# Weight bits of two halves in one operation, other due times for an inverse and a split, and no constant products

## The chip, the cores and the metric

The kernel runs on one core of a Trainium2 chip. The metric is the device time of one execution in microseconds. The kernel before took 1024.21 us, the median of three runs (1024.08 to 1024.55).

The engines have these names: PE does the matmuls (PEld is its loading of weights), DVE is the vector engine, ACT the scalar engine, POOL is GpSimd, and SP issues most DMAs. Each engine works through its own list of instructions in order, and waits where an instruction needs what another engine has not finished.

## The reference

Three stages follow each other, on 4 x 768 tokens:

```
for t in range(S):                          # attention, B=4 H=8 S=768 D=48
    kt, vt, bt = k_n[:, :, t], v[:, :, t], beta[:, :, t, None]
    y[:, :, t] = einsum('bhd,bhde->bhe', q[:, :, t], state)
    v_old = einsum('bhde,bhd->bhe', state, kt)
    state = state + bt[..., None] * einsum('bhd,bhe->bhde', kt, vt - v_old)
x = y as 3072 x 384
h = x @ w_in                                # first network, 384 x 2048
P = a[0] + a[1]*h + a[2]*h*h + a[3]*h*h*h
Q = 1 + abs(b[0])*abs(h) + abs(b[1])*h*h
x = (P / (Q + 1e-6)) @ w_out                # 2048 x 384
h = x @ w_in2; r = maximum(h, 0)            # second network
result = (r * r) @ w_out2
```

The rows k_n are k divided by its length. The weights reach the chip as 64-bit floats, and the kernel makes 32-bit floats of them.

## The kernel before

**Attention.** The recurrence is rewritten by chunks of the sequence. Each of six groups (g = 0 to 5) needs the inverse of triangular 32x32 blocks: 31 pairs of steps (L545 multiplies into tmp, L549 adds into Tt), on DVE for the first group and on POOL for the others. Then come merges of the inverses on PE (L623 and L637: products of TT, TN and ws) and bursts of small products by chunk (L734), which make the tokens' x. In the names of the order, Tt0 and Tt1, Gb0 and Gb1, vn0 and vn1 are the tiles of even and odd groups.

**First network.** The weight matrix is cut into NJ=16 tiles of 128 hidden units (j = 0 to 15), and the tokens into NT=6 passes of 512 (i). For every (i, j) there are four pieces:
- mm1 (L1021): nine products on PE, six of xh and three of xl with A (Aj), the weight as a high and a low half (A_hi, A_lo); x too is split in xh and xl (by DVE, L1005 for the second network).
- the rational: ACT makes |h| (L1044), the linear parts (L1048, L371), a logarithm (L1068) and an exponential (L1069); DVE makes the cubic and the end (L1057 to L1061); b*a is L1056 on POOL or DVE, L1054 on DVE for the first j. L1061 gives g.
- in the first pass, the products of g with B, the tile of w_out (L1105, plain). From the second pass on g is split in ph (ACT, L1078) and pl (L1079, POOL or DVE), and L1108 does products with E and F, the high and low part of B; F is B less E (L1099).
- output sums stay in banks 0 to 2 over all j.

**Weights (`weights`).** A weight tile has 768 numbers per partition, each in two 32-bit words, hi and lo: 384 of w_in (slice si) and 384 of w_out (slice so). ACT rescales hi (L959), ACT or DVE shifts lo by 29 (L960, L961). Then DVE puts the bits together, shift left by 3 and or, once per half: L969 for the in-half in place, L971 for the out-half into B. ACT copies the in-half to A_hi (L980), and a subtract gives A_lo (L981), on POOL or DVE. In the second network both halves are one operation in place (L975). Raw weights lie in the tiles raw, ra, rb and in slots called mem.

**Second network.** mm1 again, then relu and square (L1122, L1123, L1125, L1126), and products with C (L1135 to L1137). Its first mm1 follow the last products of the first network.

**What sets the order.** Nothing in the program's text does. Every instruction is a task in the class `Plan`, with an engine, an assumed duration and a due time. `run()` plays the tasks eight times: `play` takes on each engine the task that is due first among the ready ones, and `late` moves the due times backward from the end that came out. The order of the best round is issued, and is then fixed on each engine. A task made by `shared` goes to POOL or DVE, one made by `either` to ACT or DVE, as the assumed durations decide. `weights(1, j, ...)` gets its due times from tm(j), the time at which mm1 of tile j is planned. INV1 is the due time of the inverses of g from 2 on; WARM is half of the number of constant products (L458) that stand on PE at 36 to 47 us (each is two instructions in the trace); LAG1 is the distance from mm1 to the products of the same j.

Of the kernel before, what the change touches and what calls it, by code (L numbers as in the profile page):

```python
# [20 lines left out]
C = 64  # L21
# [11 lines left out]

T0, U1, U2 = 72.0, 5.55, 4.15
T2 = T0 + 96 * U1 + 3
STEP0, STEP1, INV0, INV1 = 28, 25, -90, -10
GD, GN = 26, 19
QS = (1, 1, 1, 1)
HELD = 14
OPEN = 4  # L40
BEHIND = 9
FUSE = 3
# [7 lines left out]
ROUNDS = 8  # L50
PREF, PREF2 = 1.0, 1.0
IV1, WB, WS, GW = 30, 30, 4.5, 1.2
WARM = 12
SA, SB = 40, 4


# [196 lines left out]
def kernel(ctx, tc, kT, kS, qT, kn, vn, beta, par_in, w1, w2, outT):  # L253
# [679 lines left out]
    def weights(l, j, due, duo, slack):  # L933
# [14 lines left out]
        def lo():  # L948
            return raw(rk).bitcast(U32).rearrange("p (n t) -> p n t", t=2)[:, :, 0]
# [4 lines left out]
        def res(s):  # L954
            return lo().bitcast(F32)[:, s] if f64 else raw(rk)[:, s]
        si, so = slice(0, DM), slice(DM, 2 * DM)
        if f64:
            held0 = early if l == 1 else []
            add("ACT", 0.9, lambda: A_.activation(hi().bitcast(F32), hi().bitcast(F32), AF.Prelu, scale=2.0 ** -112, alpha=2.0 ** 32), w=[(rk, 1)], due=d0, after=held0)  # L959
            fa = lambda: A_.activation(lo(), lo(), AF.Copy, scale=2.0 ** -29 * (1 - 2.0 ** -13), bias=7.5 * 2.0 ** -13 - 0.5)  # L960
            fv = lambda: V.tensor_scalar(lo(), lo(), 29, None, op0=ALU.logical_shift_right)  # L961
            if l == 1 and j in SHIFT:
                add("ACT", 0.95, fa, w=[rk], due=d0, after=held0)
            elif l == 1:
                add(("ACT", "DVE"), (0.95, 0.95), (fa, fv), lock=(0, 1), w=[rk], due=d0, after=held0)
            else:
                add("DVE", 0.95, fv, w=[rk], due=d0, lock=1)
        if f64 and l == 1:
            add("DVE", 0.7, lambda: V.scalar_tensor_tensor(lo()[:, si], hi()[:, si], 3, lo()[:, si], op0=ALU.logical_shift_left, op1=ALU.bitwise_or),  # L969
                r=[(rk, 1)], w=[rk], due=due, lock=1)  # L970
            add("DVE", 0.84, lambda: V.scalar_tensor_tensor(Bw(j).bitcast(U32), hi()[:, so], 3, lo()[:, so], op0=ALU.logical_shift_left, op1=ALU.bitwise_or),  # L971
                r=[rk, (rk, 1)], w=[("B", j)], due=duo, lock=1, free=[rk], after=over)
            last = [len(PL.tasks) - 1]
        elif f64:
            add("DVE", 1.15, lambda: V.scalar_tensor_tensor(lo(), hi(), 3, lo(), op0=ALU.logical_shift_left, op1=ALU.bitwise_or),  # L975
                r=[(rk, 1)], w=[rk], due=due, lock=1)
        elif l == 1:
            add("ACT", 0.55, lambda: A_.copy(Bw(j), res(so)), r=[rk], w=[("B", j)], due=duo, free=[rk], after=over)
            last = [len(PL.tasks) - 1]
        add("ACT", 0.52, lambda: A_.copy(Aw[j][:, si], res(si)), r=[rk], w=[("A", j)], due=due)  # L980
        shared(1.15, 0.9, lambda E: E.tensor_tensor(Aw[j][:, so], res(si), Aw[j][:, si], op=ALU.subtract),  # L981
               r=[rk], w=[("A", j)], due=due, free=[rk])
        if l == 1:
            used[rk] = last + [len(PL.tasks) - 1]
        if l == 2:
            used[rk] = [len(PL.tasks) - 1, len(PL.tasks) + 1]
            add("ACT", 0.52, lambda: A_.copy(late["C"][j][:, si], res(so)), r=[rk, "late"], w=[("C", j)], due=duo)
            add("POOL", 1.15, lambda: P_.tensor_tensor(late["C"][j][:, so], res(so), late["C"][j][:, si], op=ALU.subtract),
                r=[rk], w=[("C", j)], due=duo, lock=1, free=[rk])
            if j == 0:  # L990
                x2free[0] += [used[rk][0], len(PL.tasks) - 1]
# [181 lines left out]
    def swap():
        actx.close()
# [109 lines left out]
```

## Time and profile before

| | before |
|---|---|
| median of three runs | 1024.21 us |
| profiled execution | 1023.5 us |
| its span in the trace | 1021.7 us |
| PE busy | 969.0 us (95%) |
| DVE busy | 710.2 us (70%) |
| ACT busy | 621.3 us (61%) |
| POOL busy | 491.0 us (48%) |
| instructions | 23569 |

The profile cuts the span into 40 slices of 25.5 us; each digit is the busy share in tenths, and PEclk is the clock that PE was granted, in tenths of its full 2.4 GHz:

```profile
PE   5695999999999999999999989999999999999998
DVE  6868989998978889899769998963343433433332
POOL 3188995799879769965446976620000000000000
PEclk7677999999999999999999999999999999999999
```

The first four slices (to 102 us) hold the start of attention and of the first network; the slice at about 610 us, the 24th, holds the change from the first network to the second. In the last 15 slices POOL has nothing to do.

### The profile page before, as it was taken

The numbers are of one execution on the slowest core, as the hardware profiler recorded it, in microseconds if no ns is written. First come the engines' busy times: TensorE is split into PE (matmuls) and PEld (weight loads), VectorE is DVE, ScalarE is ACT, GpSimd is POOL, SyncE is SP. The second block draws the span as 40 slices with busy tenths as digits, with TensorE's granted clock in tenths as the row PEclk, the third lists the DMA queues.
The fourth block names the chain that finished last, engine by engine and source line by source line (L and its number), as shares of the span: only waits on it lengthen the run. The fifth ranks groups of instructions, "written<-read, shape, count | busy, mean of one in ns | idle before, by whom it ended". The sixth has DMA issues, their size and how long they took to land.

```text
span 1021.7 us, 23569 instructions
## 1 busy us (share of the span) xinstructions
PE 969.0 (95%) x9635; PEld 774.1 (76%) x9635; DVE 710.2 (70%) x1127; ACT 621.3 (61%) x1121; POOL 491.0 (48%) x609
## 2 busy tenths in 40 slices
PE   5695999999999999999999989999999999999998
PEld 4584566578777877787888867888888888888886
DVE  6868989998978889899769998963343433433332
ACT  3576878888886688678768885743232332323332
POOL 3188995799879769965446976620000000000000
PEclk7677999999999999999999999999999999999999
DMA  5975469214803541251111127300010100000000
GB/s 148 243 218 167 86 214 246 55 45 130 159 31 88 146 80 46 79 116 36 36 69 63 31 93 281 122 31 32 1 62 1 31 31 0 28 4 1 32 1 31
DMA packets 126668, 84.66 MB, mean 83 GB/s; under 512 B 95584, under 2 KB 111520, under 8 KB 126560
## 3 DMA queue, kind: packets, MB, share of 16 engines
q1 hardware_dynamic: 126560, 83.16, 29.7%
q8 instruction: 75, 1.23, 0.5%
q14 instruction: 33, 0.27, 0.1%
HBM read 63.54 MB, written 18.61 MB: 80 GB/s over the span
## 4 chain that ended last, share of the span: by engine, by line
PE 69%; POOL 13%; DVE 7%; ACT 4%; issue 3%; DMA 2%; SPq 0%; ACTq 0%; POOLq 0%; DVEq 0%
PE bank L1021 30%; PE bank L1108 10%; PE bank L734 7%; PE bank L1137 6%; PE bank L1135 6%; PE bank L1136 6%; POOL Tt L549 4%; POOL tmp L545 4%; POOL mem L1056 2%; POOL pl L1079 2%; PE bank L1105 2%; DVE mem L1061 1%; DVE bank L1060 1%; DVE mem L1059 1%; DVE mem L1057 1%
## 5 line engine op out<-in xcount | busy, mean ns | idle before, releaser
L1021 PE MATMUL bank<-xh,A 128*128 128x512 f32 (+1 forms) x1170 | 302.7, 394 | 16.7 <-DVE A L981 10.7
L1021 PEld LDWEIGHTS bank<-xh,A 128*128 128x128 f32 x1170 | 217.1, 190 | 72.1 <-DVE A L981 10.9
L1123 DVE SCALAR_TENSOR_TENSOR mem<-bank,mem 128x512 f32<-128x512 f32 x96 | 66.1, 689 | 147.4 <-ACT mem L1122 147.4
L1021 PE MATMUL bank<-xl,A 128*128 128x512 f32 (+1 forms) x585 | 163.7, 388 | 0.0
L1122 ACT ACTIVATE mem<-bank 128x512 f32<-128x512 f32 x96 | 57.4, 598 | 155.5 <-PE bank L1021 155.5
L1056 POOL TENSOR_TENSOR mem<-mem 128x512 f32<-128x512 f32 x84 | 109.7, 1307 | 49.3 <-ACT mem L1048 47.2
L1021 PEld LDWEIGHTS bank<-xl,A 128*128 128x128 f32 x585 | 110.0, 190 | 22.7
L1079 POOL TENSOR_TENSOR pl<-mem,ph 128x512 fp32r<-128x512 f32 x75 | 101.6, 1355 | 34.2 <-ACT ph L1078 25.0
L1126 DVE TENSOR_TENSOR gl<-mem,gh 128x512 fp32r<-128x512 f32 x96 | 71.8, 748 | 62.7 <-ACT gh L1125 62.6
L1137 PE MATMUL bank<-gh,C 128*128 128x512 f32 x288 | 113.7, 395 | 0.0
L1135 PE MATMUL bank<-gl,C 128*128 128x512 f32 x288 | 113.5, 394 | 0.0
L1136 PE MATMUL bank<-gh,C 128*128 128x512 f32 x288 | 111.9, 389 | 0.0
L1125 ACT CAST gh<-mem 128x512 fp32r<-128x512 f32 x96 | 59.6, 621 | 75.1 <-DVE mem L1123 62.5
L1108 PE MATMUL bank<-pl,E 128*128 128x512 f32 x240 | 99.7, 416 | 5.7 <-POOL pl L1079 5.2
L549 POOL TENSOR_TENSOR Tt<-Tt,tmp 128x31 f32<-128x31 f32 (+15 forms) x155 | 92.6, 597 | 9.4
L1108 PE MATMUL bank<-ph,F 128*128 128x512 f32 x240 | 94.8, 395 | 0.0
L1108 PE MATMUL bank<-ph,E 128*128 128x512 f32 x240 | 94.5, 394 | 0.0
L545 POOL TENSOR_TENSOR tmp<-Gb,Tt 128x31 f32<-128x31 f32 (+15 forms) x155 | 86.0, 555 | 9.7
L1068 ACT ACTIVATE mem<-mem,par 128x512 f32<-128x512 f32 x96 | 69.2, 721 | 27.5 <-POOL mem L1056 21.0
L1059 DVE SCALAR_TENSOR_TENSOR mem<-mem,par,bank 128x512 f32<-128x512 f32 x96 | 71.2, 742 | 18.1 <-ACT bank L1069 16.5
L1044 ACT ACTIVATE mem<-bank 128x512 f32<-128x512 f32 x96 | 56.8, 592 | 35.5 <-PE bank L1021 21.7
L1058 DVE SCALAR_TENSOR_TENSOR mem<-mem,par,bank 128x512 f32<-128x512 f32 x96 | 71.4, 744 | 2.1
(190 smaller groups left out, 1814.9 us busy)
## 6 DMA issues: line engine op xcount, KB each, us to landing
raw<-in_w_dram SPq DMA_DIRECT2D x17, 768.0 KB, 5.1
rb<-in_w_dram SPq DMA_DIRECT2D x8, 768.0 KB, 4.9
gs<-Gs SPq DMA_DIRECT2D x40, 128.0 KB, 3.2
X<-in_qT_dram SPq DMA_DIRECT2D x44, 112.0 KB, 2.9
kn<-in_kn_dram SPq DMA_DIRECT2D x12, 384.0 KB, 4.4
vn<-in_vn_dram SPq DMA_DIRECT2D x12, 384.0 KB, 4.5
y<-mem SPq DMA_DIRECT2D x18, 256.0 KB, 2.0
out_dram<-mem SPq DMA_DIRECT2D x18, 256.0 KB, 2.0
```

The source lines that it names most:

```text
L545: E_.tensor_tensor(tv, _mid(Gb[:, s, s + 1:32], [128, a, b]), Tt[:, 0:a, s:s + 1].to_broadcast([128, a, b]), op=ALU.mult)
L549: E_.tensor_tensor(Tt[:, 0:a, s + 1:32], Tt[:, 0:a, s + 1:32], tv, op=ALU.subtract)
L734: M.matmul(*y[:3], start=a, stop=z)
L1021: M.matmul(h, a, b, start=(m == 0), stop=(m == len(seq) - 1))
L1056: shared(1.32, 0.75, lambda E: E.tensor_tensor(b(), b(), a(), op=ALU.mult), r=[ak], w=[bk], due=due + 4.2)
L1059: q3 = lambda: V.scalar_tensor_tensor(c(), c(), s(0), h(), op0=ALU.add, op1=ALU.mult)
L1079: shared(1.3, 0.72, lambda E: E.tensor_tensor(slot[mk][0], g(), slot[pk][0], op=ALU.subtract), r=[gk, pk], w=[mk], due=due + 11.5, alloc=( ...
L1108: M.matmul(acc[d], a, b, start=(j == 0 and m == 0), stop=(j == NJ - 1 and m == 2))
L1126: add("DVE", 0.76, lambda: V.tensor_tensor(gl(), b(), gh(), op=ALU.subtract), r=[bk, gk, "late"], w=[lk], due=due + 5, lock=1, alloc=(("gl ...
L1135: M.matmul(acc[d], wh, gl, start=(j == 0), stop=False)
L1136: M.matmul(acc[d], wl, gh, start=False, stop=False)
L1137: M.matmul(acc[d], wh, gh, start=False, stop=(j == NJ - 1))
```

## The change

Five things change. First, for eleven of the sixteen weight tiles of the first network (j > 0 and j % 4 < 3) the bits of both halves are put together in one operation, 768 wide, in place of two of 384 (the branch `wide`, L973 of the new kernel). Its result goes into B: the out-half into slot j, and the in-half into slot j+1 behind it, from where ACT's copy and the subtract read it before the next tile's operation writes slot j+1. For that the two halves of w_in and w_out are stored the other way round (`w(..., True)`). The raw tile is free after the fused operation alone. Tiles 0, 3, 7, 11 and 15 keep their two operations. Second, the assumed duration of the subtract on DVE is 0.7 and not 0.9 (LOW). Third, INV1 goes from -10 to 20. Fourth, WARM is 0. Fifth, the products of the last pass are due 12 and not 18 behind mm1 (LAG0), and the split of x for the first pass of the second network is due 12 and not 4 ahead.

```diff
-STEP0, STEP1, INV0, INV1 = 28, 25, -90, -10
+STEP0, STEP1, INV0, INV1 = 28, 25, -90, 20
+LOW = 0.7
-WARM = 12
+WARM = 0
...
+        ra, rb = (so, si) if l == 1 else (si, so)
+        wide = f64 and l == 1 and j > 0 and j % 4 < 3
...
-        if f64 and l == 1:
-            add("DVE", 0.7, lambda: V.scalar_tensor_tensor(lo()[:, si], hi()[:, si], 3, lo()[:, si], op0=ALU.logical_shift_left, op1=ALU.bitwise_or),
+        if wide:
+            both = held("B", j // 4, f"Q{j // 4}", [128, 4 * DM], F32)[:, DM * (j % 4):DM * (j % 4) + 2 * DM]
+            add("DVE", 1.05, lambda: V.scalar_tensor_tensor(both.bitcast(U32), hi(), 3, lo(), op0=ALU.logical_shift_left, op1=ALU.bitwise_or),
+                r=[rk, (rk, 1)], w=[("B", j), ("B", j + 1)], due=due, lock=1, free=[rk], after=over)
+            last = [len(PL.tasks) - 1]
+        elif f64 and l == 1:
+            add("DVE", 0.7, lambda: V.scalar_tensor_tensor(lo()[:, ra], hi()[:, ra], 3, lo()[:, ra], op0=ALU.logical_shift_left, op1=ALU.bitwise_or),
                 r=[(rk, 1)], w=[rk], due=due, lock=1)
...
-        add("ACT", 0.52, lambda: A_.copy(Aw[j][:, si], res(si)), r=[rk], w=[("A", j)], due=due)
-        shared(1.15, 0.9, lambda E: E.tensor_tensor(Aw[j][:, so], res(si), Aw[j][:, si], op=ALU.subtract),
-               r=[rk], w=[("A", j)], due=due, free=[rk])
+        af = (lambda: both[:, so]) if wide else lambda: res(ra)
+        ak_ = [("B", j + 1)] if wide else [rk]
+        add("ACT", 0.52, lambda: A_.copy(Aw[j][:, si], af()), r=ak_, w=[("A", j)], due=due)
+        shared(1.15, LOW, lambda E: E.tensor_tensor(Aw[j][:, so], af(), Aw[j][:, si], op=ALU.subtract),
+               r=ak_, w=[("A", j)], due=due, free=[] if wide else [rk])
...
-    LAG1, LAG2 = 18.0, 12.0
+    LAG0, LAG1, LAG2 = 12.0, 18.0, 12.0
...
-            mm2_1(i, j, t + LAG1)
+            mm2_1(i, j, t + (LAG1 if i < NT - 1 else LAG0))
...
-        split(i, 2, due - 4)
+        split(i, 2, due - 4 if i else due - 12)
...
-    r["w1"] = w(moe_w_in[rows], moe_w_out)
+    r["w1"] = w(moe_w_in[rows], moe_w_out, True)
```

Lines from about 960 on have moved by 2 to 10: L961 is L964, L969 and L971 are L977 and L979, L980 and L981 are L990 and L991, L1021 is L1031, L1054 to L1061 are L1064 to L1071, L1079 is L1089 and L1108 is L1118 in the new kernel.

Since the order is made from durations and due times, it changes in many places. On DVE, in the first pass, these twelve instructions ended with the subtract of A2 before (mem slots hold raw weights or parts of the rational, A5 is j=5's tile):

```order
L961 TENSOR_SCALAR ra3_1088<-ra3_1088 128x768
L1054 TENSOR_TENSOR mem_102<-mem_102 128x512
L981 TENSOR_TENSOR A5_89<-raw1_107,A5_89 128x384
L677 TENSOR_TENSOR vn0_144<-vn0_144,nT1_140 128x768
L971 SCALAR_TENSOR_TENSOR B1_1285<-raw1_107 128x384
L971 SCALAR_TENSOR_TENSOR B0_898<-mem_102 128x384
L969 SCALAR_TENSOR_TENSOR ra2_993<-ra2_993 128x384
L969 SCALAR_TENSOR_TENSOR ra3_1088<-ra3_1088 128x384
L518 SCALAR_TENSOR_TENSOR nbr_138<-nbr_138,Gb0_128 128x32
L519 RECIPROCAL nbr_138<-nbr_138 128x32
L520 TENSOR_TENSOR nbr_138<-nbr_138,be_137 128x32
L981 TENSOR_TENSOR A2_86<-mem_102,A2_86 128x384
```

Now these stand around it on DVE, in the same place of the program:

```order
L991 TENSOR_TENSOR A0_84<-mem_102,A0_84 128x384
L973 SCALAR_TENSOR_TENSOR B1_179<-raw0_106 128x768
L838 TENSOR_TENSOR X2_123<-XQ2_111,bank6_75 112x4x48
L991 TENSOR_TENSOR A3_87<-mem_102,A3_87 128x384
L832 TENSOR_TENSOR xl_101<-bank7_76,xh_100 128x3x64
L838 TENSOR_TENSOR X3_124<-XQ3_112,bank5_74 112x4x48
L964 TENSOR_SCALAR ra2_984<-ra2_984 128x768
L832 TENSOR_TENSOR xl_101<-bank3_72,xh_100 128x3x64
L964 TENSOR_SCALAR ra3_1078<-ra3_1078 128x768
L991 TENSOR_TENSOR A2_86<-B0_178,A2_86 128x384
L979 SCALAR_TENSOR_TENSOR B0_178<-mem_102 128x384
L1064 TENSOR_TENSOR mem_102<-mem_102 128x512
```

The subtract of A2 comes 16 instructions earlier, counted from the same cast of x; the subtract of A5 and the scaling of vn0 have left DVE.

On POOL, where the second inverse (Tt1) ends, the third (Tt0) followed at once before:

```order
L545 TENSOR_TENSOR tmp1_133<-Gb1_129,Tt1_131 128x31
L549 TENSOR_TENSOR Tt1_131<-Tt1_131,tmp1_133 128x31
L545 TENSOR_TENSOR tmp0_132<-Gb0_128,Tt0_130 128x31
L549 TENSOR_TENSOR Tt0_130<-Tt0_130,tmp0_132 128x31
L545 TENSOR_TENSOR tmp0_132<-Gb0_128,Tt0_130 128x60
```

Now four instructions that were on DVE stand between the two inverses on POOL:

```order
L546 TENSOR_TENSOR tmp1_133<-Gb1_129,Tt1_131 128x31
L550 TENSOR_TENSOR Tt1_131<-Tt1_131,tmp1_133 128x31
L991 TENSOR_TENSOR A4_88<-B1_179,A4_88 128x384
L678 TENSOR_TENSOR vn0_144<-vn0_144,nT1_140 128x768
L678 TENSOR_TENSOR vn1_145<-vn1_145,nT1_140 128x768
L991 TENSOR_TENSOR A5_89<-B1_179,A5_89 128x384
L546 TENSOR_TENSOR tmp0_132<-Gb0_128,Tt0_130 128x31
L1066 TENSOR_TENSOR mem_102<-mem_102 128x512
```

The subtracts of A4 and A5 and both scalings of vn come behind the last step of the second inverse, and the first b*a on POOL behind the first step of the third.

On PE, at the change of the networks, the first mm1 of the second (A0) came behind the first third of j=14's products (pl0, ph0) before:

```order
L1108 MATMUL bank0_69<-pl0_2607,E3_3526 128x512
L1108 MATMUL bank0_69<-ph0_2605,F3_3643 128x512
L1108 MATMUL bank0_69<-ph0_2605,E3_3526 128x512
L1021 MATMUL bank6_75<-xh_100,A0_84 128x512 x6
L1021 MATMUL bank6_75<-xl_101,A0_84 128x512 x3
L1108 MATMUL bank1_70<-pl0_2607,E3_3526 128x512
L1108 MATMUL bank1_70<-ph0_2605,F3_3643 128x512
L1108 MATMUL bank1_70<-ph0_2605,E3_3526 128x512
```

Now two mm1 of the second network stand there on PE behind j=12's products and ahead of j=13's (pl1, ph1):

```order
L1118 MATMUL bank2_71<-ph0_2427,E3_3251 128x512
L1031 MATMUL bank6_75<-xh_100,A0_84 128x512 x6
L1031 MATMUL bank6_75<-xl_101,A0_84 128x512 x3
L1031 MATMUL bank4_73<-xh_100,A1_85 128x512 x6
L1031 MATMUL bank4_73<-xl_101,A1_85 128x512 x3
L1118 MATMUL bank0_69<-pl1_2430,E3_3251 128x512
L1118 MATMUL bank0_69<-ph1_2428,F3_3524 128x512
L1118 MATMUL bank0_69<-ph1_2428,E3_3251 128x512
```

The products of the first network that stand behind its last mm1 are now parted by mm1 of the second. In the first pass PE's order has changed too: the products of j=0 and j=1 come ahead of mm1 4, and a merge that stood ahead of mm1 6 comes behind it.

## Rows read from the trace of the kernel before

**Rows 1.** Stretches (us): length, PE, PEld, DVE, ACT, POOL busy, PEclk, DMA, GB/s

```profile
80.00:101.00 21.00, 8.91 (x57) 7.85 (x55) 17.92 (x26) 12.30 (x21) 18.87 (x33) 0.76 0.51 138
101.00:205.00 104.00, 100.36 (x1525) 64.57 (x1526) 93.83 (x151) 82.17 (x142) 81.65 (x115) 1.00 0.62 151
205.00:604.00 399.00, 392.13 (x4927) 316.58 (x4926) 348.85 (x562) 315.44 (x551) 305.87 (x353) 1.00 0.30 76
604.00:622.00 18.00, 15.07 (x58) 11.18 (x57) 17.33 (x23) 12.63 (x23) 11.32 (x10) 0.91 0.53 175
```

**Rows 2.** Waits of PE: what waited, for what, us in total, times, longest

```profile
PE bank L1021 <- DVE A L981: 10.7, 1, 10.7
...
PE bank L1108 <- POOL pl L1079: 5.2, 6, 2.0
```

**Rows 3.** Timeline of PE: start, duration, instruction, idle time before

```profile
81.11 0.52 PE L1021 MATMUL bank<-xl,A 128*128 128x256 f32 x3
92.31 1.01 PE L1021 MATMUL bank<-xh,A 128*128 128x256 f32 x3 [10.68 <-DVE A L981]
...
110.47 2.74 PE L1105 MATMUL bank<-mem,B 128*128 128x512 f32 x6
113.13 1.29 PE L623 MATMUL bank<-TT,TN 32*32 32x32 f32 x128
114.35 1.66 PE L1021 MATMUL bank<-xh,A 128*128 128x512 f32 x6
```

**Rows 4.** Timeline of DVE

```profile
91.71 0.55 DVE L981 TENSOR_TENSOR A<-mem,A 128x384 fp32r<-128x384 f32 x1
```

**Rows 5.** Groups on DVE, 58.6 to 92.4 us: count, busy us, mean ns, idle before

```profile
L971 DVE SCALAR_TENSOR_TENSOR B<-mem 128x384 uint32<-128x384 uint32 x4 | 3.7, 918 | 0.0
L969 DVE SCALAR_TENSOR_TENSOR mem<-mem 128x384 uint32<-128x384 uint32 x4 | 3.1, 774 | 0.0
...
L1054 DVE TENSOR_TENSOR mem<-mem 128x512 f32<-128x512 f32 x2 | 2.2, 1112 | 0.0
...
L981 DVE TENSOR_TENSOR A<-raw,A 128x384 fp32r<-128x384 f32 x2 | 1.5, 738 | 0.6 <-ACT A L980 0.6
...
L677 DVE TENSOR_TENSOR vn<-vn,nT 128x768 f32<-128x768 f32 x1 | 1.4, 1350 | 0.0
L961 DVE TENSOR_SCALAR raw<-raw 128x768 uint32<-128x768 uint32 x1 | 1.0, 1036 | 0.0
```

**Rows 6.** Groups on DVE in the whole span: rational, 768 wide in place

```profile
L1058 DVE SCALAR_TENSOR_TENSOR mem<-mem,par,bank 128x512 f32<-128x512 f32 x96 | 71.4, 744 | 2.1
...
L975 DVE SCALAR_TENSOR_TENSOR rb<-rb 128x768 uint32<-128x768 uint32 x8 | 10.8, 1355 | 0.3
```

**Rows 7.** Chain of waits at 211 us: start, us, what

```profile
211.08 2.05 PE bank L1021 x9
```

**Rows 8.** Timeline of POOL

```profile
64.42 0.61 POOL L545 TENSOR_TENSOR tmp<-Gb,Tt 128x240 f32<-128x240 f32 x1
...
79.00 0.92 POOL L545 TENSOR_TENSOR tmp<-Gb,Tt 128x240 f32<-128x240 f32 x1
...
100.31 0.27 POOL L549 TENSOR_TENSOR Tt<-Tt,tmp 128x31 f32<-128x31 f32 x1
...
112.75 1.01 POOL L981 TENSOR_TENSOR A<-ra,A 128x384 fp32r<-128x384 f32 x1
```

**Rows 9.** Timeline of PE at the third merge

```profile
182.70 1.01 PE L637 MATMUL bank<-ws,TN 32*32 32x32 f32 x95 [1.08 <-issue]
```

**Rows 10.** Timeline of DVE at the change of networks

```profile
611.75 2.98 DVE L1005 TENSOR_TENSOR xl<-xin,xh 128x512 fp32r<-128x512 f32 x3
```

**Rows 11.** The constant products as a group of PE

```profile
L458 PE MATMUL bank<-TT 112*128 112x256 f32 x24 | 8.5, 506 | 0.0
```

**Rows 12.** Stretches of PE alone: length, busy, PEclk, DMA, GB/s

```profile
49.00:50.00 1.00, 1.00 (x22) 0.50 1.07 305
62.00:63.00 1.00, 1.00 (x41) 0.77 0.00 0
```

More of the change, by code (lines that the diff above doesn't have):

```diff
@@ L967, in weights @@
                 add("DVE", 0.95, fv, w=[rk], due=d0, lock=1)
-        if f64 and l == 1:
-            add("DVE", 0.7, lambda: V.scalar_tensor_tensor(lo()[:, si], hi()[:, si], 3, lo()[:, si], op0=ALU.logical_shift_left, op1=ALU.bitwise_or),
+        if wide:
[5 more added lines that the diff above has]
+            add("DVE", 0.7, lambda: V.scalar_tensor_tensor(lo()[:, ra], hi()[:, ra], 3, lo()[:, ra], op0=ALU.logical_shift_left, op1=ALU.bitwise_or),
                 r=[(rk, 1)], w=[rk], due=due, lock=1)
-            add("DVE", 0.84, lambda: V.scalar_tensor_tensor(Bw(j).bitcast(U32), hi()[:, so], 3, lo()[:, so], op0=ALU.logical_shift_left, op1=ALU.bitwise_or),
+            add("DVE", 0.84, lambda: V.scalar_tensor_tensor(Bw(j).bitcast(U32), hi()[:, rb], 3, lo()[:, rb], op0=ALU.logical_shift_left, op1=ALU.bitwise_or),
                 r=[rk, (rk, 1)], w=[("B", j)], due=duo, lock=1, free=[rk], after=over)
@@ L977, in weights @@
         elif l == 1:
-            add("ACT", 0.55, lambda: A_.copy(Bw(j), res(so)), r=[rk], w=[("B", j)], due=duo, free=[rk], after=over)
+            add("ACT", 0.55, lambda: A_.copy(Bw(j), res(rb)), r=[rk], w=[("B", j)], due=duo, free=[rk], after=over)
             last = [len(PL.tasks) - 1]
-        add("ACT", 0.52, lambda: A_.copy(Aw[j][:, si], res(si)), r=[rk], w=[("A", j)], due=due)
-        shared(1.15, 0.9, lambda E: E.tensor_tensor(Aw[j][:, so], res(si), Aw[j][:, si], op=ALU.subtract),
-               r=[rk], w=[("A", j)], due=due, free=[rk])
+        af = (lambda: both[:, so]) if wide else lambda: res(ra)
[3 more added lines that the diff above has]
+               r=ak_, w=[("A", j)], due=due, free=[] if wide else [rk])
         if l == 1:
@@ L986, in weights @@
             used[rk] = [len(PL.tasks) - 1, len(PL.tasks) + 1]
-            add("ACT", 0.52, lambda: A_.copy(late["C"][j][:, si], res(so)), r=[rk, "late"], w=[("C", j)], due=duo)
-            add("POOL", 1.15, lambda: P_.tensor_tensor(late["C"][j][:, so], res(so), late["C"][j][:, si], op=ALU.subtract),
+            add("ACT", 0.52, lambda: A_.copy(late["C"][j][:, si], res(rb)), r=[rk, "late"], w=[("C", j)], due=duo)
+            add("POOL", 1.15, lambda: P_.tensor_tensor(late["C"][j][:, so], res(rb), late["C"][j][:, si], op=ALU.subtract),
                 r=[rk], w=[("C", j)], due=duo, lock=1, free=[rk])
@@ L1242, in prep_inputs, with w @@
     r = prep_attn(q, k, v, beta)
-    def w(a, b):
+    def w(a, b, c=False):
         a = a.reshape(NK, 128, NJ, 128).transpose(2, 1, 0, 3).reshape(NJ, 128, DM)
-        return np.ascontiguousarray(np.concatenate([a, b.reshape(NJ, 128, DM)], axis=2))
+        b = b.reshape(NJ, 128, DM)
+        return np.ascontiguousarray(np.concatenate([b, a] if c else [a, b], axis=2))
     r["par"] = np.ascontiguousarray(np.broadcast_to(np.concatenate([moe_a, moe_b]), (128, 6)))
```

## The prediction

> **What bounds the kernel now.** I read the table of stretches first, with the clock in it, then PE's waits, then the queues of DVE and POOL where PE stood, then single instructions for durations.
>
> The stretches [rows 1] show PE, the engine of the matmuls, busy 100.36 of 104 us between 101 and 205, 392.13 of 399 up to 604, and 15.07 of 18 at the boundary between the networks. Only 80 to 101 stands out: 8.91 of 21 us, at a mean clock of 0.76. What shortens the kernel must give PE work there, or remove the few waits behind it; work taken from another engine elsewhere lies beside a full PE.
>
> The list of PE's waits [rows 2] names them: one of 10.7 us on "DVE A L981", and six on POOL's pl, 5.2 together. The first stands ahead of the matmul group mm1 of j=2 at 92.31 [rows 3]: PE's last work before it began at 81.11 and lasted 0.52, so PE ran dry at 81.63. It lacked one subtract of 0.55 us, which DVE began at 91.71 and ended at 92.26 [rows 4]. Nothing held that but DVE's own queue, whose order is fixed: DVE was busy for 17.92 of the 21 us [rows 1].
>
> **The change part by part.** The sum is made against the profiled execution, 1023.5 us (span 1021.7). The median of the runs, 1024.21, is 0.7 above; I add that at the end.
>
> *DVE's queue ahead of A2.* From the same cast of xh on, A2's subtract is the 52nd instruction before and the 36th now. By kind, before: 8 in-half and 6 out-half operations (L969, L971), 4 shifts, 6 subtracts, 2 products of the rational (L1054), one scaling of vn (L677). Now: 2 and 1 of these, 3 fused, 5 shifts, 4 subtracts, none, none. This very stretch has their durations [rows 5]: L969 0.77 (other tiles up to 0.1 more; I take 0.80), L971 0.92 (other tiles less; 0.85), L981 0.74, L1054 1.11, L677 1.35, the shift 1.04. Gone are 6 x 0.80 + 5 x 0.85 + 2 x 0.74 + 2 x 1.11 + 1.35 = 14.1 us. A fused operation with its 768-wide result in another tile is not in this trace. Its ends: a half alone, 0.92, and the pair that it replaces, 0.92 + 0.77 = 1.69. The nearest row is the same operation, 768 wide, in place: 1355 ns over eight [rows 6]. I take 1.36. Added: 3 x 1.36 + 1.04 = 5.1 (3.8 to 6.1). Net -9.0. Three short nbr operations, 1.0 together, now stand behind A2, and one copy of TT, 0.8, has gone to ACT. So A2 is done at 92.26 - 9.0 - 1.8 = 81.5, by the ends between 80.2 and 82.5. PE ran dry at 81.63: this wait goes, but for a microsecond at most.
>
> *What is late next.* PE now has mm1 1, 2 and 3, at 2.05 for a whole one [rows 7], until about 87.4. Then it needs g, the rational's result, from DVE: along the new order, at 0.74 each [rows 6] and 1.11 where L1054 stands, g0 comes near 89, g1 near 95, g2 near 100.5. One j's products take 2.7 [rows 3]. But mm1 4 needs A4, whose subtract is now on POOL, right behind the last step of the second inverse. That step ended at 100.31 + 0.27 = 100.58, and a subtract on POOL takes 1.01 [rows 8]: A4 at 101.6. The wait has moved from DVE to POOL. Behind A4 stand two scalings of vn (1.35 on DVE [rows 5]; I allow 1.5 each on POOL) and A5, done at 105.6. PE: mm1 4 from 101.6 to 103.7, j=2's products to 106.4, mm1 5 to 108.5, j=3's products to 111.2. Then mm1 6 begins, if A6 (110.4 by the same walk along POOL) is there; before, it began at 114.35 [rows 3]. By then the new order has done one more j's products (2.7), and one piece of a merge less (L623, 1.3 [rows 3]). PE is ahead by 114.35 - 111.2 + 2.7 - 1.3 = 4.5: less than half of 10.7.
>
> Bounds. PE still waits near 88 (1.5 us), near 92 (3.5) and near 98 (3.8), and in the last the clock may fall to 1.2 GHz: three matmuls took 1.01 at that level and 0.52 at the other [rows 3]. mm1 4 and the first products behind it would then take 2.1 longer: ahead by 2.4. In the other direction, the inverse's step of one shape took POOL 0.61 us beside a quieter DVE and 0.92 beside a busy one [rows 8]. With fewer DVE instructions from 76 on, ten steps may give back 0.3 each; A4 then comes 3 us earlier: 7.5, with which the sum below would be -10.6 and the time 1013.6. I keep 4.5, since a DVE freed of the old work goes straight on to the rationals.
>
> The row, then, shows POOL slowed beside DVE, and not by what. The Trainium skill (GPSIMD Engine Reference, Key points) says that GpSimd shares its interfaces to SBUF with VectorE and contends with those of its instructions that have two SBUF inputs. By that rule only the number of such instructions counts, which falls by some ten here, and the 1013.6 would hold; the trace has no row that parts the two readings.
>
> *The third inverse, due later.* Between the two halves of its merge PE now has 19.6 us of other work instead of 2.6. The piece at 182.70 waited 1.08 [rows 9]; with so much between, it doesn't: -1.1 (0 to -1.6).
>
> *The boundary.* PE was idle for 18.00 - 15.07 = 2.9 us there [rows 1], mostly for pl of the last tiles behind POOL's queue (the longest wait, 2.0 [rows 2]). The new order runs mm1 15 right behind mm1 14, and has two mm1 of the second network ahead of the last three j, to run while pl is made. Their x is there, since its split on DVE (three of L1005, 2.98 at 611.75 [rows 10]) is due 8 us earlier. The wait goes; but the split now lies ahead of the last rationals. -3.0 (0 to -5, with the products that ran at the low clock behind the wait).
>
> *Work moved to POOL.* Over the program five b*a, five pl, five F and a subtract go from DVE to POOL, each 1.0 to 1.4 there: some 20 us, on an engine busy 305.87 of 399 [rows 1], for whose pl PE waits. +1.0 (0 to +5): PE's idle time from 205 to 604 is 6.9 us in all, and I allow one more wait of the mean size of those six. What the other eight fused operations save DVE lies beside a full PE: nothing.
>
> *The constant products.* 24 of 506 ns, 8.5 us of PE [rows 11], go. They stood beside DVE's first inverse, which ends no earlier. They had brought the clock up, but at 49 to 50 it was down at 0.50 again, and it rose in 62 to 63 [rows 12], with the chunks of the attention, which are still there. So the wide products behind them see the same clock: 0.
>
> Sum: -4.5 - 1.1 - 3.0 + 1.0 = -7.6. 1023.5 - 7.6 + 0.7 = 1016.6, told as **1016**; its own range is 1012 to 1020.
>
> **The rivals.**
> *The whole wait goes and nothing takes its place.* POOL is done early enough that A4 is there with g1. Then 10.7, 1.1 and 3.0 go, and 2.1 of the low clock behind the wait: 1007. For it: 0.61 against 0.92. Against it: POOL was busy 18.87 of these 21 us [rows 1], and the 3 us above are all I find.
>
> *The wait only moves.* A4 and A5 cost PE what A2 did; merge and boundary alone remain: 1023.5 - 4.1 + 1.0 + 0.7 = 1021. For it: A4's place behind a whole inverse that runs until 100.58. Against it: three j's products that PE can now do before and between.
>
> *The clock stays low.* Without the constant products PE could be at 1.2 GHz until the half-wide products near 75: 12.5 us of work from 62.5 on, up to 5.8 us longer, of which the wait for A4 takes a part: 1018 to 1020. For it the Trainium skill (TensorE: Matmul & The Clock Gate, "Why this matters for your kernels") says to warm the engine with matmuls and to leave no idle gaps between bursts. Against it: the clock at 49, soon after they had run [rows 12].
>
> *Slower.* In B's tile the in-half of a weight lies in the slot of the next out-half, which the next fused operation writes: DVE must wait, in order, until ACT and POOL have read it. Eight fused operations stand behind a subtract on POOL, itself among the inverse's steps (0.61) and b*a (1.3): each up to 1.9 late, 15.2 together, with the rationals queued behind. If DVE's idle 10.2 us of 104 [rows 1] take up half of their own length, 5.1, PE gets 10.1 of it; the first gain is lost, 4.1 stays: 1023.5 + 10.1 - 4.1 + 0.7, about 1030. It decides from where A4 comes later than 104. Against it: a tile's chain of 1.36, some 0.5 on ACT and 1.01 is short beside the 7 us from one mm1 to the next.
>
> That the change doesn't do what it says would be a fused operation as long as its pair, 1.69: A2 comes 1.0 later, which the wait for A4 covers.
>
> **How the numbers follow.** Forecast 0.47 (0.12 of it for the 1013.6 of a quicker POOL), the whole wait 0.17, only moved 0.15, low clock 0.08, slower 0.13. A measurement of this kernel can tell about 0.2%, 2 us, from no change. "Slower" is the last rival, 0.13; a third of "only moved" lies within 2 us, 0.05; faster is the rest, 0.82. The range is 1006 to 1022.5: outside lie the slower case and a little below 1007, under 0.2.
>
> **What would show it.** Right: no wait for A2, its subtract done near 81.5; waits near 88, 92 and 98, the last released by POOL's A at about 101; mm1 6 near 111; no wait ahead of the third merge; at most 1 us at the boundary; the fused operation at 1.36. Wrong: A4 from POOL before 98 or after 104; the clock at 0.5 past 63; new waits of PE on POOL or DVE between 205 and 604.

## The result and the profile after

The changed kernel takes 1008.1 us (median of four runs, 1006.9 to 1008.75) against 1024.4 of the kernel before: a ratio of 0.9845, with a 95% interval of 0.9825 to 0.9866. The forecast was 1016, with a range of 1006 to 1022.5; the gain is twice the forecast one. The profiled execution took 1008.75 us, with a span of 1007.0, 14.7 less than before.

The table of stretches after (length, PE, PEld, DVE, ACT, POOL busy, PEclk, DMA, GB/s), to be read against [rows 1]:

```profile
80.00:101.00 21.00, 15.84 (x105) 11.14 (x101) 19.74 (x32) 18.87 (x29) 18.09 (x32) 1.00 0.35 102
101.00:205.00 104.00, 99.96 (x1472) 66.02 (x1473) 93.59 (x147) 79.65 (x144) 94.17 (x125) 0.98 0.60 154
205.00:604.00 399.00, 392.27 (x5019) 319.60 (x5006) 337.75 (x552) 318.77 (x560) 319.33 (x365) 1.00 0.32 81
604.00:622.00 18.00, 18.00 (x78) 13.99 (x78) 16.86 (x21) 13.87 (x26) 11.30 (x9) 1.00 0.76 258
```

PE has 15.84 us of work in the stretch that held 8.91, and the boundary's 18 us are full. In the two stretches between, its idle time is what it was, although POOL has 12.5 and 13.5 us more to do.

PE's timeline after, from the first half of mm1 2 on, answers to [rows 3]:

```profile
83.80 0.88 PE L1031 MATMUL bank<-xh,A 128*128 128x256 f32 x6
...
89.58 2.84 PE L1115 MATMUL bank<-mem,B 128*128 128x512 f32 x6 [1.39 <-DVE mem L1071]
95.04 2.84 PE L1115 MATMUL bank<-mem,B 128*128 128x512 f32 x6 [1.71 <-DVE mem L1071]
99.94 2.03 PE L1031 MATMUL bank<-xh,A 128*128 128x512 f32 x6 [2.06 <-POOL A L991]
101.77 1.49 PE L1031 MATMUL bank<-xl,A 128*128 128x512 f32 x3
103.05 3.46 PE L1115 MATMUL bank<-mem,B 128*128 128x512 f32 x6
105.94 1.95 PE L1031 MATMUL bank<-xh,A 128*128 128x512 f32 x6
...
110.59 1.95 PE L1031 MATMUL bank<-xh,A 128*128 128x512 f32 x6
```

There is no wait for A2. Three short ones have come: for g0 at 89.58, for g1 at 95.04, for A4 from POOL at 99.94. The matmuls behind the last run longer (1.49 for three, then 0.86): after PE's 2.06 us of idling the clock fell to 1.2 GHz for a moment (PE alone: length, busy, PEclk, DMA, GB/s):

```profile
101.00:103.00 2.00, 2.00 (x6) 0.52 0.55 139
```

The mm1 and the products under it took 6.00 us, from 99.94 to 105.94; the next pair took 4.65. On DVE the subtract of A2, which began at 91.71 before [rows 4], stands here:

```profile
82.17 0.98 DVE L991 TENSOR_TENSOR A<-B,A 128x384 fp32r<-128x384 f32 x1
```

and POOL's own timeline has A4 behind the inverse's last step, the two scalings, and A5 ([rows 8] before):

```profile
98.66 0.27 POOL L550 TENSOR_TENSOR Tt<-Tt,tmp 128x31 f32<-128x31 f32 x1
98.88 1.01 POOL L991 TENSOR_TENSOR A<-B,A 128x384 fp32r<-128x384 f32 x1
99.84 3.63 POOL L678 TENSOR_TENSOR vn<-vn,nT 128x768 f32<-128x768 f32 x2
103.44 1.00 POOL L991 TENSOR_TENSOR A<-B,A 128x384 fp32r<-128x384 f32 x1
```

**Where the 14.7 us come from.** The same instruction in both traces tells how far PE is ahead. mm1 of j=6 in the first pass starts at 110.59 instead of 114.35; with one j's products more (2.7) and a merge less (1.3) done, that is 5.2. A mm1 in the fourth pass, behind all attention, and one near the end of the second network (PE's timeline of before, then of after):

```profile
442.87 0.39 PE L1021 MATMUL bank<-xh,A 128*128 128x512 f32 x1
...
1000.09 1.08 PE L1021 MATMUL bank<-xh,A 128*128 128x512 f32 x4
```

```profile
433.88 0.39 PE L1031 MATMUL bank<-xh,A 128*128 128x512 f32 x1
...
985.39 0.86 PE L1031 MATMUL bank<-xh,A 128*128 128x512 f32 x3
```

9.0 us ahead in the one, 14.7 in the other. So the first stage gave 5.2, the middle passes 3.8, the boundary 5.7. From 433.88 to 985.39 it is 551.5 us, where it was 557.2. Of the 5.7, 0.6 came late in the last pass and not at the boundary: the mm1 at 589.54, 599.09 before, is 9.6 ahead. These are single traces, good to a microsecond or two: the trace of experiment 1, whose time is that of the kernel before, is 1.4 ahead at the end, and that of experiment 4, whose time is that of the changed kernel, 16.5.

### The profile page after: what moved, and what is told of

It reads as the page before. It is cut to its first block, busy times and chain, and to the rows that moved or that the text cites. A ratio compares the mean times of both kernels' runs of the same rounds, so it can differ in the third digit from the quotient of the medians.

```text
span 1007.0 us, 23528 instructions
## 1 busy us (share of the span) xinstructions
PE 958.9 (95%) x9611; PEld 770.5 (77%) x9611; DVE 686.4 (68%) x1100; ACT 617.3 (61%) x1121; POOL 510.0 (51%) x625
## 4 chain that ended last, share of the span: by engine, by line
PE 72%; POOL 15%; DVE 3%; ACT 3%; issue 3%; SPq 2%; DMA 1%; POOLq 0%; ACTq 0%; DVEq 0%
PE bank L1031 31%; PE bank L1118 11%; PE bank L735 7%; PE bank L1147 7%; PE bank L1145 7%; PE bank L1146 7%; POOL Tt L550 3%; POOL pl L1089 3%; POOL tmp L546 3%; POOL mem L1066 3%; SPq L357 2%; PE bank L638 1%; POOL A L991 1%; PE bank L1115 1%; PE bank L624 1%
## 5 line engine op out<-in xcount | busy, mean ns | idle before, releaser
L1031 PE MATMUL bank<-xh,A 128*128 128x512 f32 (+1 forms) x1170 | 301.5, 393 | 3.4 <-POOL A L991 3.1
L1031 PEld LDWEIGHTS bank<-xh,A 128*128 128x128 f32 x1170 | 217.6, 189 | 56.6 <-POOL A L991 6.7
L1031 PE MATMUL bank<-xl,A 128*128 128x512 f32 (+1 forms) x585 | 163.3, 388 | 0.0
L1066 POOL TENSOR_TENSOR mem<-mem 128x512 f32<-128x512 f32 x89 | 117.0, 1315 | 51.0 <-ACT mem L1058 46.7
L1031 PEld LDWEIGHTS bank<-xl,A 128*128 128x128 f32 x585 | 109.8, 189 | 22.6
L1089 POOL TENSOR_TENSOR pl<-mem,ph 128x512 fp32r<-128x512 f32 x80 | 106.4, 1330 | 22.4 <-ACT ph L1088 22.3
L1118 PE MATMUL bank<-pl,E 128*128 128x512 f32 x240 | 98.9, 412 | 6.9 <-POOL pl L1089 6.9
L1118 PE MATMUL bank<-ph,E 128*128 128x512 f32 x240 | 94.2, 393 | 0.0
L1118 PE MATMUL bank<-ph,F 128*128 128x512 f32 x240 | 94.2, 393 | 0.0
L1069 DVE SCALAR_TENSOR_TENSOR mem<-mem,par,bank 128x512 f32<-128x512 f32 x96 | 71.3, 743 | 29.4 <-ACT bank L1079 28.3
L1054 ACT ACTIVATE mem<-bank 128x512 f32<-128x512 f32 x96 | 56.9, 593 | 42.3 <-PE bank L1031 32.7
L1067 DVE TENSOR_TENSOR mem<-bank,mem 128x512 f32<-128x512 f32 x96 | 65.7, 684 | 12.0 <-ACT mem L372 11.4
```

The lines of the kernel that those rows point to most:

```text
L1031: M.matmul(h, a, b, start=(m == 0), stop=(m == len(seq) - 1))
L1066: shared(1.32, 0.75, lambda E: E.tensor_tensor(b(), b(), a(), op=ALU.mult), r=[ak], w=[bk], due=due + 4.2)
L1069: q3 = lambda: V.scalar_tensor_tensor(c(), c(), s(0), h(), op0=ALU.add, op1=ALU.mult)
L1089: shared(1.3, 0.72, lambda E: E.tensor_tensor(slot[mk][0], g(), slot[pk][0], op=ALU.subtract), r=[gk, pk], w=[mk], due=due + 11.5, alloc=( ...
L1118: M.matmul(acc[d], a, b, start=(j == 0 and m == 0), stop=(j == NJ - 1 and m == 2))
```

## The experiments

Ratios are to the kernel before, with 95% intervals; the changed kernel stands at 0.9845 [0.9825, 0.9866]. The edits of 1 and 2 are made to the kernel before, all others to the changed kernel. Most edits make the planner order much anew, so each order was read before the run; where one instruction alone is moved, that is said.

**1. The constant products alone.**
```diff
-WARM = 12
+WARM = 0
```


> The kernel before without the 24 constant products (8.5 us of PE at 36 to 47 us); every other instruction keeps its place. Theory A (they lie beside the first inverse on DVE, and the clock they bring is gone again at 49): no change, 1023.5 to 1025; the clock rises at 60 to 63 with the chunks as before. Rival B (the clock stays at 1.2 GHz longer without them, up to the half-wide products at 75): 1026 to 1028, with the first half-products of mm1 at half speed. Rival C (their 8.5 us delay the attention): 1020 or less.

Measured: 1023.81 us, 1.0001 [0.9985, 1.0018]. Theory A. PE's clock (length, busy, PEclk, DMA, GB/s) rose between 59 and 60 us, no later than before [rows 12]:

```profile
59.00:60.00 1.00, 1.00 (x54) 0.78 0.84 344
```

From 60 on it stood at 2.4 GHz (1.00 in 60 to 61). PE was busy with the attention's small products throughout both microseconds.

**2. The two due times at the boundary alone.**
```diff
-    LAG1, LAG2 = 18.0, 12.0
+    LAG0, LAG1, LAG2 = 12.0, 18.0, 12.0
-            mm2_1(i, j, t + LAG1)
+            mm2_1(i, j, t + (LAG1 if i < NT - 1 else LAG0))
-        split(i, 2, due - 4)
+        split(i, 2, due - 4 if i else due - 12)
```


> The kernel before with only the two due times at the change of the networks (products of the last pass 12 behind mm1, first split of the second network 12 ahead). Theory A (the two waits on pl, the wait on A of the second network behind them and the low clock at 612 to 615 all hang on this order): 5 to 6 us faster, 1018.5. Rival B (my term of 3.0 was right, and the rest of what the changed kernel gains there comes from weights or POOL work that moved for another reason): 1021 to 1021.5.

Measured: 1020.7 us, 0.9975 [0.9958, 0.9992]. The times lie nearer to B; the trace nearer to A: of the waits behind 580 us, one of 1.8 for pl is left, and the same two mm1 as above are 552.8 us apart (443.28 to 996.07), 4.4 less than before. Between the 2.6 of the times and this 4.4 the runs can't decide (they spread over 6 us).

**3. The fused operation alone** (the changed kernel with all else set back: WARM 12, INV1 -10, LOW 0.9, both due times at the boundary).
```diff
-STEP0, STEP1, INV0, INV1 = 28, 25, -90, 20
+STEP0, STEP1, INV0, INV1 = 28, 25, -90, -10
-LOW = 0.7
+LOW = 0.9
-WARM = 0
+WARM = 12
-            mm2_1(i, j, t + (LAG1 if i < NT - 1 else LAG0))
+            mm2_1(i, j, t + LAG1)
-        split(i, 2, due - 4 if i else due - 12)
+        split(i, 2, due - 4)
```


> The kernel before with the fused operation alone (constants, due time of the inverses, assumed 0.9 of the subtract and both due times at the boundary as before). A2's subtract is then 18 instructions earlier on DVE, and those of A4 and A5 are on POOL among the first steps of the third inverse. Theory A (the wait for A2 goes and a shorter one for A4 comes): 4 to 6 us faster, 1018 to 1020, no wait of 10.7, mm1 of j=4 at 100 to 104. Rival B (DVE waits in order for POOL's subtracts through the slots of B): 1026 or more, with waits of DVE L973 on POOL's A of over 1 us each. Rival C (the first gain comes from the inverse's due time, not from the fused operation): 1023 to 1025.

Measured: 1015.99 us, 0.9927 [0.9905, 0.995]: more than A, in its direction. PE's waits in this kernel, from 75 to 700 us (total, times, longest):

```profile
PE bank L1118 <- POOL pl L1089: 6.4, 6, 2.0
PE bank L1031 <- POOL A L991: 6.3, 4, 3.9
```

The 10.7 us are gone; 3.9 are paid to POOL for one A. DVE's fused operations waited for POOL's A twice, 3.4 us together, so the chain through B's slots exists, and is short.

**4. The same order, but pairs for the fused operations** (nothing else moves).
```diff
-            add("DVE", 1.05, lambda: V.scalar_tensor_tensor(both.bitcast(U32), hi(), 3, lo(), ...),
+            add("DVE", 1.05, lambda: [V.scalar_tensor_tensor(both[:, s].bitcast(U32), hi()[:, s], 3, lo()[:, s], ...) for s in (so, si)],
```


> The changed kernel with each of the eleven fused operations issued as two of 384 that write the same places; every instruction stands where it stood. It tells the shorter operation from the new order. Theory A (the order and the place of the subtracts make the gain; PE's waits near 88 and 93 and the full PE behind hide 0.3 to 0.5 us per pair): 1008 to 1010. Rival B (the fused operation's own time makes it): three pairs ahead of A2 make its subtract a microsecond later, DVE misses about 5 us in all, 1012 or more.

Measured: 1007.75 us, 0.9846 [0.9819, 0.9873]. Theory A. The groups of the two kernels, the changed one first (count, busy us, mean ns):

```profile
L973 DVE SCALAR_TENSOR_TENSOR B<-raw 128x768 uint32<-128x768 uint32 x8 | 12.8, 1604 | 0.1
L973 DVE SCALAR_TENSOR_TENSOR B<-mem 128x768 uint32<-128x768 uint32 x2 | 2.1, 1052 | 0.0
```

```profile
L973 DVE SCALAR_TENSOR_TENSOR B<-raw 128x384 uint32<-128x384 uint32 x16 | 15.7, 1022 | 0.0
L973 DVE SCALAR_TENSOR_TENSOR B<-mem 128x384 uint32<-128x384 uint32 x4 | 3.3, 870 | 0.0
```

With the one tile in ra, eleven fused operations take 15.8 us, their pairs 20.1. DVE as a whole is busy 689.9 us and not 686.4, 3.5 more, and the kernel is no slower. The saved DVE time is not the gain; the order is.

**5. The inverses' due time back.**
```diff
-STEP0, STEP1, INV0, INV1 = 28, 25, -90, 20
+STEP0, STEP1, INV0, INV1 = 28, 25, -90, -10
```


> The changed kernel with the inverses of the groups from 2 on due at -10 again, as before. On POOL the subtracts of A4 and A5 and the work of the rationals then stand behind steps of the third inverse, and this is spread over POOL earlier. Theory A (the due time gives the middle passes their gain, PE was 3 to 4 us further ahead at the fourth pass than at the first, and part of the first stage's): 1011 to 1014. Rival B (it is worth the one merge that waited 1.08 and 0.54): 1009.5. Rival C (the fused operation and its order bring it all): 1008.

Measured: 1012.5 us, 0.9886 [0.9866, 0.9906], as theory A has it, but in the first stage and not in the middle passes. PE's timeline of this kernel:

```profile
110.42 2.15 PE L1031 MATMUL bank<-xh,A 128*128 128x512 f32 x6 [3.42 <-POOL A L991]
```

With the third inverse due early, its steps stand ahead of A5 on POOL: A5 came at 110.36 where it came at 104.44, and mm1 5 waited 3.42. The middle passes gain what they gain in the changed kernel: the mm1 that the kernel before starts at 210.92 and 451.03 start here at 208.61 and 445.05, 2.3 and 6.0 ahead, and in the changed kernel at 205.63 and 442.04, 5.3 and 9.0 ahead, 3.7 between the two in both.

**6 and 7. The boundary's due times back, both, then the one of the products alone.**
```diff
-            mm2_1(i, j, t + (LAG1 if i < NT - 1 else LAG0))
+            mm2_1(i, j, t + LAG1)
-        split(i, 2, due - 4 if i else due - 12)      # in 6 alone
+        split(i, 2, due - 4)
```


> The changed kernel with both due times at the change of the networks as before; nothing ahead of 570 us moves but a few late instructions. Theory A (PE's lead grows from 9.6 at the last j to 14.7 in the second network by this order): 1012.5 to 1013.5. Rival B (the term of 3.0): 1011. Rival C (as the same edit gave the kernel before, 2.6 by its times): 1010.7.

Measured: 1013.84 us, 0.9893 [0.9873, 0.9914]. Theory A. PE waits behind 570 us for two different things in this kernel:

```profile
PE bank L1118 <- POOL pl L1089: 2.9, 2, 2.0
PE bank L1031 <- POOL A L991: 1.9, 2, 1.6
```

> The changed kernel with the products of the last pass due 18 behind mm1 again, and the split of x for the second network early as in the changed kernel. On PE two mm1 of the second network then still stand ahead of j=13's products, but mm1 of j=15 comes behind j=11's products again. It tells which of the two due times the gain at the boundary hangs on. Theory A (the mm1 of the second network, which need the early split, fill PE while pl is made): 1008 to 1010, one wait of at most 2 us for pl between 590 and 605, no wait on A of the second network. Rival B (mm1 15 right behind mm1 14 makes pl of the last tiles early): 1012 to 1014, two waits for pl.

Measured: 1012.75 us, 0.9895 [0.9869, 0.9921]: rival B by the time, and three waits for pl of 3.9 together; the wait for A is gone. From the mm1 in the fourth pass to the one at the end it is 556.7 us in experiment 6, 554.2 here, 551.5 in the changed kernel: by the traces the early split is worth 2.5 and the earlier products 2.7. By the times the split alone is worth nothing that is clear of the noise (0.9895 against 0.9893). The earlier products without the early split were not run.

**8. No fusion.**
```diff
-        wide = f64 and l == 1 and j > 0 and j % 4 < 3
+        wide = False
```


> The changed kernel with no fused tiles: both halves in two operations for all sixteen, raw tiles free after both, and the order that follows from it. A2's subtract stands ten instructions earlier on DVE than with the fusion, A1's is on POOL, A4's and A5's stay on DVE. Theory A (the place of the subtracts in DVE's queue made the gain, since issuing the fused operations as pairs cost nothing): 1008 to 1012, no wait of over 3 us near 81. Rival B (the fusion is the gain by the raw tiles and slots that come free earlier): 1016 or more.

Measured: 1016.77 us, 0.9929 [0.9909, 0.9949], beyond A. The planner now puts A1 on POOL among the inverse's steps, and PE waits for it (its waits from 84 to 600 us):

```profile
PE bank L1118 <- POOL pl L1089: 6.2, 6, 2.2
PE bank L1031 <- POOL A L991: 2.6, 1, 2.6
```

With experiment 4 this says: the fusion pays by what the planner can then place where. Rival B's reason, tiles that come free earlier, was not parted from that.

**9. A4 and A5 forced on DVE.**
```diff
-        shared(1.15, LOW, lambda E: ...
+        sh = (lambda a, b, f, **k: add("DVE", b, lambda: f(V), lock=1, **k)) if l == 1 and j in (4, 5) else shared
+        sh(1.15, LOW, lambda E: ...
```


> The changed kernel with the subtracts of A4 and A5 put on DVE: A4's stands right behind A2's, A5's 16 further on. It takes the wait for A4 (2.06 us at 97.9) out of POOL's queue. Theory A (POOL's place behind the second inverse sets when mm1 of j=4 starts): mm1 of j=4 starts near 92 to 95 and not at 99.9, and 1 to 3 us are won: 1005 to 1007. Rival B (PE waits there for DVE's rationals in any case, and the two subtracts make these 1.6 us later): 1008 to 1009, the wait goes to g1 and g2.

Measured: 1019.48 us, 0.9961 [0.9943, 0.9979]. Both theories missed. The planner moved the end of g0's rational behind A5 on DVE, and one wait of 11.96 us for g0 came in place of the three short ones. It tells nothing on A4, but shows how much one place in DVE's queue is worth.

**10 and 11. A4's subtract moved by hand on POOL, all else in place; then the scalings of vn behind A5 too.**
```diff
+        o.remove(m["A", 4])                       # in the finished order
+        o.insert(o.index(m["nrm2"]), m["A", 4])   # ahead of the third norm
+        for x in (m["vn", 3], m["vn", 2]):        # in 11 alone
+            o.remove(x)
+            o.insert(o.index(m["A", 5]) + 1, x)
```


> The changed kernel with one instruction moved by hand and no other: A4's subtract goes on POOL from behind the second inverse's last step to ahead of the norm of the third (where POOL waited 0.94 for ACT at 91.4). Theory A (its place on POOL sets the start of mm1 of j=4): the wait of 2.06 at 97.9 goes, mm1 4 starts at 97.9 and not 99.9, mm1 5 at about 103.5 when A5 is done, and 1 to 2 us stay: 1006 to 1007.5. Rival B (A5, A6 and the rationals behind it bind just as much): mm1 6 at 110.5 as before and no gain, 1008.

Measured: 1008.33 us, 0.9842 [0.9828, 0.9855]: no gain clear of the noise, as rival B has it, though the interval still holds the 1007.5 of theory A. The wait for A4 went as A had it, and others took its place (PE's waits from 84 to 112 us):

```profile
PE bank L1126 <- DVE mem L1082: 5.7, 3, 2.0
PE bank L1042 <- POOL A L1002: 1.5, 1, 1.5
```

PE's first mm1 began 3.6 us earlier in this trace than in the changed kernel's (71.28 against 74.90), ahead of everything that the edit moves, so the sizes of its waits compare only roughly.

> As the one before, and the two scalings of vn on POOL (3.63 us together in the changed kernel) stand behind A5's subtract and not ahead of it. Theory A: A5 is done near 102.5 and not at 104.4, the fused operation of j=5 no longer runs beside a scaling and takes 1 to 1.4 us where it took 2.22; mm1 5 starts near 102.7, 2 to 3 us stay: 1005 to 1006.5. Rival B (POOL stands idle for A5's copy and the scalings delay b*a of j=4 and the third inverse by as much): 1008 or more.

Measured: 1010.61 us, 0.9858 [0.9845, 0.9872]: rival B. POOL stood 2.84 us for ACT's half of A5, and mm1 6 waited for A6 instead:

```profile
PE bank L1046 <- POOL A L1006: 2.4, 1, 2.4
```

So what is late behind A2 is not one instruction: DVE's rationals and POOL's row of subtracts end close together.

**12. The assumed duration of the subtract.**
```diff
-LOW = 0.7
+LOW = 0.9
```


> The changed kernel with 0.9 assumed again for the subtract on DVE. The order of the first tiles is nearly the same (A2's subtract stands two places earlier on DVE, A4's and A5's stay on POOL); later ones differ. Theory A (this number is one of many that shake the order, without a mechanism of its own): within 3 us of the changed kernel on either side, its waits for pl at other places. Rival B (it is worth a part of the middle passes' gain): 1010 to 1013.

Measured: 1016.07 us, 0.9913 [0.9899, 0.9927]: 8 us slower than the changed kernel, more than either theory gave. In the first stage nothing is lost. At 270 and 281 PE waits for pl:

```profile
269.96 0.79 PE L1118 MATMUL bank<-pl,E 128*128 128x512 f32 x1 [1.68 <-POOL pl L1089]
...
281.02 0.79 PE L1118 MATMUL bank<-pl,E 128*128 128x512 f32 x1 [3.04 <-POOL pl L1089]
```

and between 268 and 288 the granted clock was 0.74 on the mean, with 15.28 us of PE busy; in the changed kernel 0.91 and 17.20. A number that touches only the subtracts moved the rationals and the inverse's steps on POOL of the second pass. The two mm1 of experiment 5 start here at 205.40 and 449.04, 5.5 and 2.0 ahead of the kernel before: the middle passes lose 3.5 where they gained 3.7.

No experiment gave a version that beats the changed kernel clearly.

## Why the prediction was right or wrong

- *A2's queue*: the wait went, as forecast, but A2 came late. Forecast 81.5, by the ends 80.2 to 82.5; measured 83.15, past the later end. The durations were not at fault: the three fused operations ahead of it took 1.15, 0.95 and 1.40 (1.36 assumed). The sum had durations alone, and the shorter queue ran into more waits: from the same cast of xh on, DVE waited 5.1 us for PE and ACT where it had waited 3.5. Two of the seven (DVE's timeline after):

```profile
72.75 0.35 DVE L838 TENSOR_TENSOR X<-XQ,bank 112x192 f32<-112x192 f32 x1 [1.19 <-PE bank L735]
...
79.56 0.36 DVE L832 TENSOR_TENSOR xl<-bank,xh 128x192 fp32r<-128x192 f32 x1 [0.70 <-ACT xh L372]
```

  PE didn't wait because mm1 0 and 1 ended later too, at 83.96. Had they ended at 81.63 as before, PE would have waited 1.5 us: that part is luck.
- *What is late next*: right in mechanism; the size is near because two misses offset each other. Forecast g0 near 89, g1 near 95, g2 near 100.5, A4 at 101.6, mm1 6 at 111.2, and 4.5 us ahead; measured 89.5, 95.0, 99.3, 99.9, 110.59 and 5.2. POOL's inverse ended at 98.93 instead of 100.58, inside the bound that I gave for a DVE with fewer instructions, and A4 came 1.7 earlier. Then the clock fell behind the wait for A4, which I had put among the bounds and not into the sum, and took 1.35 of it back (6.00 against 4.65), so that mm1 6 was only 0.6 earlier. That A4 itself is the bound was too narrow (10 and 11).
- *The third inverse, -1.1, and the work moved to POOL, +1.0*: these terms were mis-sized. The middle passes gave 3.8. The fear behind the +1.0 was right as far as it goes: waits for pl from 101 to 580 us rose from 2.0 to 5.1, which I had named as a sign of being wrong. But the other waits fell by more, in PE's list for 101 to 580 us, before and then after:

```profile
PE bank L637 <- issue: 4.0, 3, 1.7
PE bank L1021 <- DVE mem L1061: 2.4, 4, 1.5
PE bank L1108 <- POOL pl L1079: 2.0, 3, 1.1
```

```profile
PE bank L1118 <- POOL pl L1089: 5.1, 5, 2.4
PE bank L638 <- issue: 1.7, 2, 1.0
PE bank L1031 <- POOL A L991: 1.0, 1, 1.0
```

  I had priced one of the three merges, by the order around it, and left the waits on DVE's g out. And the due time of the inverses is worth 3 us by the traces and 4 by the times in the first stage (5), where it keeps the third inverse from standing ahead of A5; I had priced it in the middle passes alone, which gain as much without it. What they hang on is the order that goes with the subtract's 0.7: with 0.9 they lose 3.5 (12). I had given that number no term. Between the mm1 at 110.59 and 433.88, idle time explains 1.7 of the 3.8 (8.3 us, 10.0 before), and the products counted as done ahead or behind match; of the rest 1.3 shows as mm1 that kept PE busy 125.67 us and not 126.94, and I can't lay it to one cause.
- *The boundary, -3.0*: mis-sized; 5.7, just over its bound of 5. One wait of 1.8 for pl is left, so the waits for pl gave only 1.1. Another 1.9 is the wait for the second network's A on POOL, which I had not looked for behind 622 us. Behind the longest wait for pl the clock was low before (PE alone):

```profile
612.00:615.00 3.00, 2.96 (x8) 0.50 0.52 162
```

  That cost about 1.5, an estimate: half of the 2.96 us. After, it is 2.4 GHz throughout (1.00 from 604 to 622). With the 0.6 of the last pass this makes 5.1; the rest is open. Experiments 6 and 7 show that the gain needs the earlier products; whether these need the early split was not run.
- *The constant products, 0*: right (1).
- *The rivals*: the low clock is refuted by experiment 1. The chain through B's slots shows in experiment 3 at 3.4 us and not in the changed kernel. The sum's own range, 1012 to 1020, misses the 1008.1; the stated one holds it only because it was drawn down to 1006 for the rival "the whole wait goes", and that is luck. This rival has nearly the measured time, 1007, by the wrong way: of the 12.8 us that it gave to the first stage 5.2 came there, the rest in the middle passes and at the boundary. "Only moved" is refuted by the 5.2 and by the time.

So the direction and the first stage followed from the profile; half of the gain came from terms set too small, and the order of a planner that is shaken as a whole was priced as if each edit kept to its own place.

## What to carry to other kernels

Where a queue in fixed order holds one short instruction that the bound engine waits for, count what stands ahead of it by kind and duration, and then walk the next two or three things that the bound engine needs, on each engine: here that gave every event of the first stage to 2 us. Add the waits of that engine for others: in the shorter queue they grew from 3.5 to 5.1 us. Saved time on an engine that is not the bound was worth nothing (3.5 us, experiment 4), while one assumed number, which moves the order, was worth 8 (experiment 12). And look for the waits of a boundary behind it as well as at it: the second network's first weights waited there too.

## What the runs showed of the hardware

An instruction of DVE with both inputs in SBUF (where all tiles of this kernel lie that are not banks) and one of POOL seem to take turns: the one that starts second is longer by what is left of the first. The fused operation of j=5 took 2.22 us in the changed kernel (DVE's timeline), where it began 0.08 behind POOL's first scaling of vn:

```profile
99.92 2.22 DVE L973 SCALAR_TENSOR_TENSOR B<-raw 128x768 uint32<-128x768 uint32 x1
```

In experiment 11 the same operation had no scaling beside it, and the next one began 0.06 ahead of a b*a on POOL (DVE's timeline, then POOL's):

```profile
100.01 0.95 DVE L986 SCALAR_TENSOR_TENSOR B<-raw 128x768 uint32<-128x768 uint32 x1
...
105.54 0.95 DVE L986 SCALAR_TENSOR_TENSOR B<-ra 128x768 uint32<-128x768 uint32 x1
```

```profile
105.60 2.03 POOL L1081 TENSOR_TENSOR mem<-mem 128x512 f32<-128x512 f32 x1
```

DVE, first, takes 0.95 both times; POOL's b*a, second, takes 2.03 where the mean of the changed kernel is 1.31. The scalings took 3.63 together in the changed kernel and 2.92 in experiment 11. And in experiment 9 a subtract of DVE, of a form that takes 0.99 on the mean in the changed kernel, began 0.21 behind a product of 2.34 on POOL:

```profile
94.00 2.54 DVE L992 TENSOR_TENSOR A<-B,A 128x384 fp32r<-128x384 f32 x1
```

Two inputs are not needed: the shift has one, and took 1.00 us in the changed kernel where it began 0.02 behind a step of the inverse (0.60 at 81.22 on POOL), and 0.56 a moment earlier (DVE's timeline):

```profile
80.09 0.56 DVE L964 TENSOR_SCALAR ra<-ra 128x768 uint32<-128x768 uint32 x1
...
81.24 1.00 DVE L964 TENSOR_SCALAR ra<-ra 128x768 uint32<-128x768 uint32 x1
```

The rational's operations with an input in a bank ran beside POOL's long product in the changed kernel (2.38 at 94.19) at 0.65 to 0.75, as everywhere. This agrees with the Trainium skill (GPSIMD Engine Reference, Key points), which names DVE instructions with two SBUF inputs, or in a 2-port perf mode, as contending with GpSimd. Whether the shift runs in such a mode no run here shows. That the later one pays is what these places show, and no run was made for it alone.
